# Two linear-attention and MLP layers on one core: the first tile's mean from two engines, two tiles by halves, and five new instruction lists

## The chip, the cores and the metric

The kernel runs on one core of a Trainium2 chip. A core has five engines with an instruction stream of their own each: TensorE (PE in the profile) multiplies matrices into eight PSUM banks, VectorE (DVE), ScalarE (ACT) and GpSimd (POOL) do elementwise work, and SyncE (SP) issues most of the DMAs. The engines wait for each other only by semaphores. The metric is the device time of one execution in microseconds. The kernel before takes 326.31 us, the median of 3 runs (325.96 to 327.42).

## The reference

`x` is 2048 tokens by 512 channels, in bf16. Two attention blocks alternate with two MLP blocks, and both layers share the same weights:

```
phi = lambda t: where(t > 0, t + 1, exp(t)) + 1e-6
def A(x):                                  # linear attention, 32 heads of 16
    q, k, v = split(x @ wqkv)              # wqkv: 512 x 1536
    pq, pk = phi(q), phi(k)
    kv  = einsum("bhsd,bhse->bhde", pk, v)
    z   = einsum("bhsd->bhd", pk)
    num = einsum("bhqd,bhde->bhqe", pq, kv)
    den = einsum("bhqd,bhd->bhq", pq, z)[..., None] + 1e-6
    return (num / den) @ wo                # wo: 512 x 512
def B(x):                                  # MLP, 512 -> 1792 -> 512
    return gelu(layernorm(x) @ w1 + b1) @ w2 + b2

x = x + A(layernorm(x));  x = x + B(layernorm(x))
x = x + A(layernorm(x));  x = x + B(layernorm(x))
```

`layernorm` subtracts the mean over the 512 channels and divides by `sqrt(var + 1e-5)`.

## The kernel before

The 2048 tokens are 16 tiles of 128, in four chunks of four tiles. Chunk 3 (tiles 12 to 15) is worked first, then chunks 0, 1 and 2. Every piece of work is an operation with a name, an engine, the keys that it reads and writes, and the buffers it uses. For each engine the configuration at the top of the file (`ORDER` in `CONF`, line 345) holds a list of all its operations by name, written out; the engines run these lists in that order, and a planner (`Scheduler`, line 114) only goes through them with estimated durations to give buffers to the operations. `WAY` says for some operations which engine or method does them. A wait is put in wherever an operation reads what another engine, or a DMA, has still to write, or takes a buffer that another has still to give up. So the five lists set which work can overlap, and an operation whose turn has not come waits even if its data are there.

In the names the first digit is the layer (0 or 1; in the names of the first norm it stands behind A, in those of the second behind B), the last ones are the tile, or the chunk and a part. What stands around the change:

- DMA loads on SP: `x0` (tiles 12 and 13), `wk0` and `wk1` (the two halves of the q and k weights, split along the 512 channels that are summed over), `x2` (tiles 14 and 15), then `xc0` to `xc2` (the other chunks). `wv`, `wo` and four pieces of `w1` and `w2` follow later on GpSimd's queue.
- `norm` (line 713). A tile's mean and variance come from two VectorE instructions, `stats` (bn_stats, line 741, over 512 channels) and `aggr` (line 743). `veps` adds eps, `pow` (GpSimd, line 756) raises to -1/2. For tiles 12 to 15 of layer 0 the mean is subtracted at once (`cen`, line 722, into the buffer `yb`), and the tile goes on to its transpose without 1/std; that factor (`rstd`) is applied where q and k are read out of PSUM, and to `yb` itself later, by `ysc` (lines 763 and 766). The other tiles have both in one instruction, `norm` (line 776 on ScalarE, with `nmr` ahead of it on GpSimd; line 781 on VectorE).
- The transpose: `PT` is four TensorE transposes (`transpose_pe`, line 795) and `tc` the copy out of PSUM; tile 12's are done by halves, two transposes and a copy each (lines 804 and 811). Other tiles go by a DMA transpose (`TA`, `TB`, `TP` on SP, lines 791 and 1120).
- `K0_t` and `Q0_3_k` are the k and q projections of a tile, four matmuls of 128 x 128 by 512 each (lines 878 and 908). For tile 12 they are two pairs (`K0_12_0` then `K0_12`, line 887; `Q0_3_0_0` then `Q0_3_0`, line 917), the first for the first half of the weights. `Q` of chunks 0 and 1 in layer 0 works on all four tiles of a chunk (line 934).
- phi of a projection: `exp` and `relu` on ScalarE (lines 848 and 859), `min` and `phi` on VectorE (lines 861 and 865; lines 852 and 854 where phi is a maximum and no relu is needed), some `phi` on GpSimd.
- `G` multiplies the normed tile by phi(k) (line 1004, in four PSUM banks that are held for all of layer 0), so that K and Q have the other four banks until then. `za` adds phi(k) for z on GpSimd (zacc, line 957); `zhi`, `zlo` and `ZH` (lines 963, 966 and 973) turn it into a column; `Z` does the same for whole chunks (line 985). `cpg`, `KV`, `kvm`, `M` and `cpm` make one 512 x 512 matrix of it all, `D`, `ln`, `rec`, `pr` divide by the denominator, `WO` (line 1152) multiplies, and `RA` adds the residual.
- `statsB` to `normB` is the second norm; `W1Lc_f_h` the up-projection of a chunk (line 1184; chunk 0 by halves of two tiles), `gelu` on ScalarE (line 1190), `W2L_t_0` and `W2L_t_7` the two halves of a tile's down-projection (line 1223), `RB` the residual, `OD` the store.

Between `exp` and `gelu` ScalarE loads another table (line 1356), 11 times in the list before. At the start TensorE runs matmuls on constants (`warm`, line 703), and a few more between the first transposes (`idle0_0` and `idle0_1`, as many as `N_IDLE` says).

Of the kernel before, what the change touches and what calls it, by code (L numbers as in the profile page):

```python
# [7 lines left out]
ACT = mybir.ActivationFunctionType  # L8
ALU = mybir.AluOpType

P = 128
# [271 lines left out]
def assign_waits(graph, order, sems, dma_sems):  # L283
# [10 lines left out]
    while len(done) < total:  # L294
        moved = False
        for e in ENGINES:
# [43 lines left out]
    N_WARM2=9, N_IDLE=[2, 1], XQ='sp', WKQ='sp sp', WK1=1, K_SPLIT=1, K_HALVES=(0, 1), X_HEAD=((0, 2), (2, 2)),  # L340
# [204 lines left out]
def build_kernel(nc, A_x, A_wqkv, A_wo, B_x, B_w1, B_b1, B_w2, B_b2, out, conf=None, report=False):  # L545
# [5 lines left out]
    with ExitStack() as es:  # L551
# [161 lines left out]
        def norm(src, src_keys, src_tiles, double, on_act, prio, tag, src16=False, head=False):  # L713

            s = Tile(STATS, f"st{tag}")
            k = f"st{tag}"
            by_act = eng(f"st{tag}") == "act"
            centred = eng(f"cen{tag}") is not None

            def centre(mean, op):  # L720
                y = Tile(YB, f"y{tag}")
# [698 lines left out]
```

## Time and profile before

| what | us |
|---|---|
| median of 3 runs (lowest, highest) | 326.31 (325.96, 327.42) |
| the profiled execution's own time | 326.6 |
| its span, from the first to the last instruction | 324.9 |
| busy in the span: TensorE | 319.8 |
| busy: VectorE | 224.4 |
| busy: ScalarE | 193.7 |
| busy: GpSimd | 144.6 |

The granted clock is 1.00 in all of the span. Matmuls overlap in the array, and a matmul's end is modelled, so TensorE's busy time counts some standing still; the starts of its matmuls are the better measure. Times in the timeline count from the span's start. In the answer by stretches the columns are the stretch and its length, the busy time and instructions of TensorE's matmuls, its weight loads, VectorE, ScalarE and GpSimd, then the granted clock, the DMA engines' share and GB/s. An idle time in square brackets stands before the instruction, with what ended it.

### The profile page before, as it was taken

How to read it: one execution, taken by the hardware profiler on the slowest of the kernel's cores; microseconds unless marked ns; L12 is line 12 of the kernel's file. 1: busy time of each engine (PE TensorE's matmuls, PEld its weight loads, DVE VectorE, ACT ScalarE, POOL GpSimd, SP SyncE). 2: the span in 40 equal slices, each digit the busy share in tenths (PEclk: the TensorE clock that was granted, in tenths of full speed). 3: DMA queues.
4: the chain of work that ended last, by engine and by line, in shares of the span. 5: the costliest groups of instructions: out<-in, count | busy, mean ns of one | idle time of the engine just before them, and what ended most of it. 6: DMA issues, size and time to landing. Idle time of an engine off the chain costs nothing.

```text
span 324.9 us, 4758 instructions
## 1 busy us (share of the span) xinstructions
PE 319.8 (98%) x1703; PEld 157.9 (49%) x1703; DVE 224.4 (69%) x508; ACT 193.7 (60%) x333; POOL 144.6 (45%) x231
## 2 busy tenths in 40 slices
PE   7999999999999999999999999999999999999996
PEld 3444445567444444444444444558644444444443
DVE  4998979997998854003779999899899666100032
ACT  3999699745253235899527656978934734563300
POOL 4699476646522862500346825755904543100000
PEclk9999999999999999999999999999999999999999
DMA  7343179003331221210110300121230421300012
GB/s 259 144 64 72 40 236 355 18 16 76 40 64 35 58 57 32 43 22 17 34 33 16 67 17 0 18 48 36 41 72 18 82 65 50 81 0 15 31 65 69
DMA packets 46355, 20.37 MB, mean 63 GB/s; under 512 B 42044, under 2 KB 44220, under 8 KB 46332
## 3 DMA queue, kind: packets, MB, share of 16 engines
q1 hardware_dynamic: 45132, 15.32, 20.6%
q0 software_dynamic: 1056, 4.72, 4.1%
q8 instruction: 13, 0.21, 0.3%
q14 instruction: 10, 0.08, 0.1%
q10 hardware_dynamic: 144, 0.03, 0.0%
HBM read 8.00 MB, written 2.10 MB: 31 GB/s over the span
## 4 chain that ended last, share of the span: by engine, by line
PE 88%; DVE 4%; POOL 3%; DMA 2%; issue 1%; ACT 0%; SPq 0%
PE ps L1184 30%; PE ps L1223 29%; PE ps L1152 9%; PE ps L878 5%; PE ps L1036 4%; PE ps L908 4%; PE ps L1004 2%; PE ps L934 2%; DMA t<-in_A_x_dram 2%; DVE stats L741 1%; POOL rstd L756 1%; PE ps L1210 1%; PE ps L1128 1%; POOL zacc L957 1%; DVE yb L781 1%
## 5 line engine op out<-in xcount | busy, mean ns | idle before, releaser
L1190 ACT ACTIVATE gT<-ps,b1c 128x512 bf16<-128x512 f32 (+1 forms) x140 | 76.9, 600 | 70.9 <-PE ps L1184 70.6
L1184 PE MATMUL ps<-t,w 128*128 128x512 bf16 (+1 forms) x560 | 102.6, 336 | 0.0
L1223 PE MATMUL ps<-w,gT 128*128 128x512 bf16 x434 | 98.2, 379 | 0.0
L1184 PEld LDWEIGHTS ps<-t,w 128*128 128x128 bf16 x560 | 54.5, 98 | 43.9 <-ACT t L833 0.6
L1223 PEld LDWEIGHTS ps<-w,gT 128*128 128x128 bf16 x434 | 42.5, 98 | 50.5 <-ACT gT L1190 0.2
L848 ACT ACTIVATE eb<-ps 128x512 bf16<-128x512 f32 x56 | 32.8, 608 | 17.2 <-PE ps L878 10.6
L756 POOL TENSOR_TENSOR rstd<-veps,neghalf 128x1 f32<-128x1 f32 x64 | 38.7, 615 | 5.6 <-DVE veps L754 3.2
L1233 DVE TENSOR_TENSOR pkb<-ps,xsb 128x512 bf16<-128x512 f32 x15 | 10.0, 682 | 32.8 <-PE ps L1223 32.7
L741 DVE BATCH_NORM_STATS2 stats<-xsb 128x6 f32<-128x512 f32 x48 | 32.2, 681 | 0.2
L878 PE MATMUL ps<-wqkv,t 128*128 128x512 bf16 x124 | 31.2, 379 | 0.0
L1229 DVE TENSOR_TENSOR xsb<-ps,xsb 128x512 f32<-128x512 f32 x16 | 10.9, 686 | 29.2 <-PE ps L1223 29.2
L1152 PE MATMUL ps<-gtb,t 128*128 128x512 bf16 x128 | 30.7, 379 | 0.0
L754 POOL TENSOR_SCALAR veps<-mv 128x1 f32<-128x1 f32 x29 | 8.3, 297 | 39.1 <-DVE mv L743 38.4
L859 ACT ACTIVATE rb<-ps 128x512 bf16<-128x512 f32 x38 | 22.7, 612 | 2.0 <-PE ps L878 1.5
L776 ACT ACTIVATE yb<-xsb,nmr,rstd 128x512 bf16<-128x512 f32 x21 | 16.8, 812 | 10.8 <-POOL nmr L773 10.8
L781 DVE TENSOR_SCALAR yb<-xsb,mv,rstd 128x512 bf16<-128x512 f32 x27 | 15.3, 574 | 10.1 <-POOL rstd L756 9.9
L1169 POOL TENSOR_TENSOR xsb<-xsb,b2b 128x512 f32<-128x512 f32 x14 | 17.6, 1258 | 5.4 <-DVE yb L781 4.9
L1116 POOL TENSOR_TENSOR t<-t,rr 128x512 bf16<-128x512 bf16 x7 | 7.7, 1100 | 26.2 <-DVE rr L1112 16.5
L746 POOL TENSOR_SCALAR veps<-mv 128x1 f32<-128x1 f32 x32 | 10.2, 319 | 20.6 <-DVE mv L743 18.8
L1152 PEld LDWEIGHTS ps<-gtb,t 128*128 128x128 bf16 x128 | 12.4, 98 | 14.0
L908 PE MATMUL ps<-wqkv,t 128*128 128x512 bf16 x76 | 19.2, 379 | 0.0
L878 PEld LDWEIGHTS ps<-wqkv,t 128*128 128x128 bf16 x124 | 11.8, 98 | 14.5 <-ACT rb L859 0.6
(102 smaller groups left out, 415.9 us busy)
## 6 DMA issues: line engine op xcount, KB each, us to landing
w<-in_B_w_dram POOLq DMA_DIRECT2D x4, 896.0 KB, 7.2
out_dram<-pkb SPq DMA_DIRECT2D x15, 128.0 KB, 2.0
t<-in_A_x_dram SPq DMA_DIRECT2D x3, 512.0 KB, 7.3
wqkv<-in_A_wqkv_dram SPq DMA_DIRECT2D x2, 512.0 KB, 4.6
t<-yb SPq DMA_TRANSPOSE x56, 2.5
t<-in_A_x_dram SPq DMA_DIRECT2D x2, 256.0 KB, 4.2
wqkv<-in_A_wqkv_dram POOLq DMA_DIRECT2D x1, 512.0 KB, 4.4
wo<-in_A_wo_dram POOLq DMA_DIRECT2D x1, 512.0 KB, 5.1
```

What stands on the lines that cost most here:

```text
L741: G.op("dve", lambda e: e.bn_stats(stats[:, s.slot, :], src()), 602, reads=src_keys, writes=[k + "s"], tiles=[s, *src_tiles], prio=prio, n ...
L756: G.op("pool", lambda e: e.tensor_tensor(rstd[:, s.slot:s.slot + 1], veps[:, s.slot:s.slot + 1], neghalf[:], op=ALU.pow), 530, reads=[k + ...
L781: G.op("dve", lambda e: e.tensor_scalar(yb[:, y.slot, :], src(), stats[:, s.slot, 2:3] if by_act else mv[:, s.slot, 0:1], rstd[:, s.slot:s ...
L848: G.op("act", lambda e: e.activation(eb[:, et.slot, :], bank(bt), ACT.Exp, scale=factor()), 569 if by else 483, reads=[src_key, *more], wr ...
L859: G.op("act", lambda e: e.activation(rb[:, rt.slot, :], bank(bt), ACT.Relu, scale=factor()), 569 if by else 478, reads=[src_key, *more], w ...
L878: ins = e.matmul(bank(b), lhsT=yTa(yT)[:, dt, k * P:(k + 1) * P], rhs=wqkv[:, dt, D:2 * D], start=(dt == 0), stop=(dt == DT - 1))
L908: ins = e.matmul(bank(b), lhsT=yTa(yT)[:, dt, k * P:(k + 1) * P], rhs=wqkv[:, dt, 0:D], start=(dt == 0), stop=(dt == DT - 1))
L1152: ins = e.matmul(bank(wb), lhsT=yTa(pq)[:, kt, k * P:(k + 1) * P], rhs=gtb[:, kt, :], start=(kt == 0), stop=(kt == DT - 1))
L1169: G.op("pool" if on_pool else "dve", lambda e: e.tensor_tensor(xsb[:, st, :], xsb[:, st, :], b2b[:], op=ALU.add), 1120 if on_pool else 600 ...
L1184: ins = e.matmul(bank(b, n), lhsT=w1[:, dt, ft * P:(ft + 1) * P], rhs=yTa(yT)[:, dt, k0 * P:k1 * P], start=(dt == 0), stop=(dt == DT - 1))
L1190: G.op("act", lambda e, ft=ft, b=b, k0=k0, k1=k1, n=n: e.activation(gT[:, g.slot, ft * 512 + k0 * P:ft * 512 + k1 * P], bank(b, n), ACT.Ge ...
L1223: ins = e.matmul(bank(b), lhsT=gT[:, g.slot, ft * 512 + k * P:ft * 512 + (k + 1) * P], rhs=w2[:, ft, :], start=(ft == 0), stop=(ft == FT - 1))
```

## The change

Three settings of the configuration change: `K_SPLIT` from 1 to 2, `N_IDLE` from `[2, 1]` to `[4, 1]`, and `WAY` has `stA0_12` as "both" and `stA0_13` as "sum" (it was "dve" for tile 13).

With "both", tile 12's mean is taken ahead of its statistics: ScalarE sums channels 256 to 511 (`sumA0_12`, a copy that also accumulates), VectorE sums channels 0 to 255 (`redA0_12`), VectorE adds the two and multiplies by -1/512 (`negA0_12`), and the mean is added to the tile by two instructions of 256 channels each (`cenA0_12_0`, `cenA0_12_1`), so that each half can be transposed by itself. With "sum", ScalarE sums all of tile 13 (`sumA0_13`), VectorE scales it (`negA0_13`), and one `cen` follows. `stats`, `aggr`, `veps` and `pow` come after that in both and serve for `rstd` alone. `K_SPLIT=2` makes tile 13's projections two pairs of matmuls as well (`K0_13_0`, `K0_13`, `Q0_3_1_0`, `Q0_3_1`).

The five lists are replaced. On TensorE 390 names become 392, on ScalarE 322 become 324, on VectorE 508 become 512; GpSimd's and SP's hold the same names in another order. All other names are the same, permuted. The start of TensorE's list, and the code:

```diff
-    N_WARM2=9, N_IDLE=[2, 1], XQ='sp', WKQ='sp sp', WK1=1, K_SPLIT=1, K_HALVES=(0, 1), X_HEAD=((0, 2), (2, 2)),
+    N_WARM2=9, N_IDLE=[4, 1], XQ='sp', WKQ='sp sp', WK1=1, K_SPLIT=2, K_HALVES=(0, 1), X_HEAD=((0, 2), (2, 2)),
...
-            "warm PTA0_12_0 PTA0_12_1 idle0_0 PTA0_13 idle0_1 K0_12_0 K0_12 Q0_3_0_0 Q0_3_0 K0_13 PTA0_14 Q0_3_1 "
-            "PTA0_15 K0_14 G0_12_0 K0_15 Q0_3_2 Q0_3_3 G0_13_0 PTA0_1 K0_0 G0_14_0 K0_1 G0_15_0 G0_0_0 K0_3 K0_2 "
...
+            "warm PTA0_12_0 PTA0_12_1 idle0_0 Q0_3_0_0 PTA0_13 idle0_1 Q0_3_0 K0_12_0 K0_12 Q0_3_1_0 Q0_3_1 K0_13_0 "
+            "PTA0_14 K0_13 PTA0_15 K0_14 K0_15 Q0_3_3 G0_12_0 G0_13_0 Q0_3_2 K0_0 PTA0_1 G0_14_0 K0_3 K0_1 G0_15_0 "
+            "G0_0_0 K0_2 Q0_0_0 Q0_0_3 G0_1_0 Q0_0_2 G0_2_0 K0_10 K0_8 K0_5 K0_4 G0_3_0 Q0_0_1 K0_6 K0_7 K0_9 G0_4_0 "
+            "Q0_1_3 K0_11 Q0_1_2 ZH0 G0_5_0 Z0_1 Z0_2 Q0_1_1 Q0_1_0 D0_0_3 G0_6_0 D0_0_0 G0_7_0 G0_8_0 D0_0_1 G0_9_0 "
...
-        "pz1_3_1": "dve", "pz1_3_2": "pool", "pz1_3_3": "pool", "stA0_13": "dve", "tc_10": "act", "tc_11": "dve",
+        "pz1_3_1": "dve", "pz1_3_2": "pool", "pz1_3_3": "pool", "stA0_12": "both", "stA0_13": "sum", "tc_10": "act", "tc_11": "dve",
...
+            early = eng(f"st{tag}") if eng(f"st{tag}") in ("both", "sum") else None
...
+                if early == "both":
+                    halves = cf["K_HALVES"]
+                    n = D // len(halves)
+                    G.parts[f"y{tag}"] = tuple(f"y{tag}_{h}" for h in halves)
+                    for h in halves:
+                        cs = slice(n * h, n * h + n)
+                        G.op("dve", lambda e, cs=cs: e.tensor_scalar(yb[:, y.slot, cs], src()[:, cs], mean(), None, op0=op), 180,
...
-            if by_act:
+            if early:
...
+                h0 = D // 2 if early == "both" else 0
+                G.op("act", lambda e: e.activation(eb[:, et.slot, h0:D], src()[:, h0:D], ACT.Copy, accum_out=st6(0)), 450 if h0 else 630,
...
+                if h0:
+                    G.op("dve", lambda e: e.tensor_reduce(st6(3), src()[:, 0:h0], axis=mybir.AxisListType.X, op=ALU.add), 330, reads=src_keys,
...
+                    G.op("dve", lambda e: e.tensor_scalar(st6(2), st6(0), st6(3), -1.0 / D, op0=ALU.add, op1=ALU.mult), 75,
...
+                else:
+                    G.op("dve", lambda e: e.tensor_scalar(st6(2), st6(0), -1.0 / D, None, op0=ALU.mult), 75,
...
+                y = centre(lambda: st6(2), ALU.add)
+                G.op("dve", lambda e: e.bn_stats(stats[:, s.slot, :], src()), 602, reads=src_keys, writes=[k + "s", k + "t", k + "m"],
...
-                    o = G.op("pe", turn, n * 66, reads=[ykey, f"id{P}"], writes=[f"{key}_{h}p"], tiles=[bs[h], y], prio=prio, name=f"PT{tag}_{h}",
+                    o = G.op("pe", turn, n * 66, reads=[f"{ykey}_{h}" if ykey in G.parts else ykey, f"id{P}"], writes=[f"{key}_{h}p"], tiles=[bs[h], y], prio=prio, name=f"PT{tag}_{h}",
...
-                    if f"yT{L}_{4 * c + k}" in G.parts:
+                    if L == 0 and c == HC and k < cf["K_SPLIT"]:
```

The other places that the prediction speaks of, in the new lists:

- VectorE begins with `ones redA0_12 negA0_12 cenA0_12_0 cenA0_12_1 negA0_13 statsA0_12 cenA0_13 aggrA0_12 vepsA0_12 statsA0_13 aggrA0_13 yscA0_12 statsA0_14`; `yscA0_13` stands behind `aggrA0_1`. Further on it has `normA0_11 mink0_4 phik0_4 minq0_0_1 mink0_5 mink0_7 phik0_5 mink0_6 phik0_7 zhi0 mink0_9 zlo0`.
- ScalarE begins with `sumA0_12 sumA0_13 tcA0_12_0 tcA0_12_1 tcA0_13 reluq0_3_0 expq0_3_0 reluk0_12 expk0_12 tcA0_14 expk0_13 tcA0_15`. It has 9 table changes. At the end of layer 1's first chunk it has `gelu1_0_4_1 normB1_6 gelu1_0_9_1 gelu1_0_2_1 normB1_4 gelu1_0_6_1 expq1_2_2 expq1_2_3 gelu1_0_10_1 normB1_7`, where the list before had `gelu1_0_6_0 normB1_4 gelu1_0_10_1 gelu1_0_5_1 expq1_2_3 expq1_2_2 gelu1_0_0_1 gelu1_0_8_1 normB1_6 normB1_7`.
- TensorE there goes `W11_0_9_1 W21_1_0 W21_0_0 W21_1_7 W21_0_7 W21_3_0 W21_3_7 WO1_12_0 W11_1_13_0`; before it did four tiles of `W21` and three `WO` ahead of `W11_1`.
- GpSimd: `bdm0` stands between `vepsA0_13` and `powA0_13` (it was first), `bdm1` behind `za0_1` (it was fifth), `b1z` behind `pr0_1_0`, and the DMA `w1_1` behind `pr0_1_1`.
- SP: the seven loads come first as before; then `TA0_0 TA0_3 TA0_2 TA0_5 TA0_10 TA0_8 TA0_4 TA0_7 TA0_6 TA0_9 TA0_11 b1 Tb1 TB0_1 TB0_3 TB0_2 b2` (before: `b1` behind `TA0_8`, `b2` ahead of `TB0_1`).

More of the change, by code (lines that the diff above doesn't have):

```diff
@@ L724, in centre @@
                 return y
[L725 removed]
+            if early:
+                et = Tile(EB, f"sq{tag}")
+                st6 = lambda i: stats[:, s.slot, i:i + 1]
+                h0 = D // 2 if early == "both" else 0
+                G.op("act", lambda e: e.activation(eb[:, et.slot, h0:D], src()[:, h0:D], ACT.Copy, accum_out=st6(0)), 450 if h0 else 630,
+                     reads=src_keys, writes=[k + "s"], tiles=[s, et, *src_tiles], prio=prio, name=f"sum{tag}", lat=90)
+                if h0:
+                    G.op("dve", lambda e: e.tensor_reduce(st6(3), src()[:, 0:h0], axis=mybir.AxisListType.X, op=ALU.add), 330, reads=src_keys,
+                         writes=[k + "t"], tiles=[s, *src_tiles], prio=prio, name=f"red{tag}", lat=40)
+                    G.op("dve", lambda e: e.tensor_scalar(st6(2), st6(0), st6(3), -1.0 / D, op0=ALU.add, op1=ALU.mult), 75,
+                         reads=[k + "s", k + "t"], writes=[k + "m"], tiles=[s], prio=prio, name=f"neg{tag}", lat=40)
+                else:
+                    G.op("dve", lambda e: e.tensor_scalar(st6(2), st6(0), -1.0 / D, None, op0=ALU.mult), 75,
+                         reads=[k + "s"], writes=[k + "m"], tiles=[s], prio=prio, name=f"neg{tag}", lat=40)
+                y = centre(lambda: st6(2), ALU.add)
+                G.op("dve", lambda e: e.bn_stats(stats[:, s.slot, :], src()), 602, reads=src_keys, writes=[k + "s", k + "t", k + "m"],
+                     tiles=[s, *src_tiles], prio=prio, name=f"stats{tag}", lat=50)
+                G.op("dve", lambda e: e.bn_aggr(mv[:, s.slot, :], stats[:, s.slot, :]), 92, reads=[k + "s"], writes=[k + "a"],
+                     tiles=[s], prio=prio, name=f"aggr{tag}", lat=55)
+                head = eng(f"veps{tag}") == "dve"
+                G.op("dve" if head else "pool",
+                     lambda e: e.tensor_scalar(veps[:, s.slot:s.slot + 1], mv[:, s.slot, 1:2], EPS, None, op0=ALU.add),
+                     75 if head else 182, reads=[k + "a"], writes=[k + "v"], tiles=[s], prio=prio, name=f"veps{tag}", lat=50)
+            elif by_act:
                 et = Tile(EB, f"sq{tag}")
```

10 lines of the change are left out of this document (7 added, 3 removed), and 268 rows, old and new, of the table ORDER.

## The prediction

> **What bounds the kernel now.** I read the page's busy line first, then the busy time by stretches, then TensorE's own timeline, and then, for each place where TensorE stood still, the waits.
>
> ```profile
> PE 319.8 (98%) x1703; PEld 157.9 (49%) x1703; DVE 224.4 (69%) x508; ACT 193.7 (60%) x333; POOL 144.6 (45%) x231
> ```
>
> ```profile
> 12.00:16.00 4.00, 4.00 (x20) 1.79 (x19) 3.97 (x11) 4.00 (x9) 3.70 (x7) 1.00 0.16 33
> 20.00:25.00 5.00, 5.00 (x25) 2.27 (x24) 4.93 (x15) 4.92 (x9) 4.54 (x10) 1.00 0.34 69
> 30.00:35.00 5.00, 4.30 (x21) 1.69 (x19) 4.76 (x8) 2.75 (x6) 3.83 (x5) 1.00 0.33 67
> 60.00:100.00 40.00, 40.00 (x245) 23.40 (x244) 36.15 (x80) 20.46 (x42) 19.20 (x25) 1.00 0.26 47
> ```
>
> TensorE (first busy column) is full; until 35 us VectorE and ScalarE (third and fourth) are nearly full beside it, later they have room. A busy TensorE may still lose time, so I go by the starts of its matmuls:
>
> ```profile
> 5.34 0.57 PE L804 MATMUL ps<-idp,yb 128*128 128x128 bf16 x4 [0.40 <-DVE yb L722]
> 5.74 0.28 PE L697 MATMUL ps<-const-bfloat16-1.0 128*128 128x128 bf16 x2
> 5.86 0.38 PE L823 MATMUL ps<-idp,yb 128*128 128x128 bf16 x4
> 6.21 0.60 PE L887 MATMUL ps<-wqkv,t 128*128 128x512 bf16 x2
> 7.40 0.59 PE L887 MATMUL ps<-wqkv,t 128*128 128x512 bf16 x2 [0.58 <-DMA wqkv<-in_A_wqkv_dram]
> 7.83 1.03 PE L917 MATMUL ps<-wqkv,t 128*128 128x512 bf16 x4
> 8.69 1.03 PE L878 MATMUL ps<-wqkv,t 128*128 128x512 bf16 x4
> 9.75 0.40 PE L823 MATMUL ps<-idp,yb 128*128 128x128 bf16 x4
> ```
>
> ```profile
> 33.16 1.03 PE L878 MATMUL ps<-wqkv,t 128*128 128x512 bf16 x4
> 34.89 0.39 PE L1004 MATMUL ps<-pkb,yb 128*128 128x512 bf16 x1 [0.70 <-DVE pkb L854]
> ```
>
> From 7.83 to 8.69 four 512-wide matmuls take 0.86 us: the pace is 0.216 each. At that pace the two at 6.21 end at 6.64, but the next start at 7.40: 0.75 us waiting for the second half of the weights (wk1). The four at 8.69 end at 9.55 and tile 14's transposes start at 9.75: 0.20 lost. The four at 33.16 end at 34.02 and the next start at 34.89: 0.86 lost. Going so through the whole timeline I find four losses of 0.04 to 0.08 between 19 and 33 us (0.26), and 0.06 at 74.3; after that none. So past 7.40 TensorE loses 1.38 us in all; before 7.40 it has done 0.43 us of matrix work (K0_12's first half) and some transposes.
>
> ```profile
> PE ps L1004 <- DVE pkb L854: 0.7, 1, 0.7
> PE ps L887 <- DMA wqkv<-in_A_wqkv_dram: 0.6, 1, 0.6
> ```
>
> Behind the longest loss stands VectorE: ahead of the one that TensorE waited for (L854), normA0_11 took 1.31 where its kind takes 0.41, while GpSimd added zacc (32.93 to 34.08). The last line is zlo0, which matters below:
>
> ```profile
> 32.92 1.31 DVE L781 TENSOR_SCALAR yb<-t,mv,rstd 128x512 bf16<-128x512 bf16 x1
> 34.15 0.68 DVE L854 SCALAR_TENSOR_TENSOR pkb<-ps,eb 128x512 bf16<-128x512 f32 x1
> 37.50 1.26 DVE L966 TENSOR_TENSOR eb<-zacc,dz 128x512 bf16<-128x512 f32 x1
> ```
>
> The sum is made against the profiled execution: span 324.9, device time 326.6, so 1.7 outside the span, 0.3 above the median 326.31.
>
> **1. The first tile's mean ahead.** Removed: the wait of cenA0_12 for both bn_stats and their aggregates (3.52 to 4.94). Added: sumA0_12 (ScalarE, 256 wide), redA0_12 (VectorE, 256 wide), two neg, one more cen, sumA0_13 (ScalarE, 512). None but cen is in the trace. sumA0_12: 0.38 by the 256-wide copy of L811, 0.82 by the 512-wide SBUF copy of L763; half of the latter, 0.41, is nearest. redA0_12: half of L1107's 0.675, 0.34, beside it; bounds 0.15 (smallest VectorE row) and 0.68. neg 0.15 each (L754). A cen half: 0.15 to 0.34 (L722). x lands at 3.52, so the first transposes could go at 4.2 to 4.9; TensorE's warm-up ends at 4.73, so 4.8 instead of 5.34. On VectorE the stats of 12 and 13 move behind, and cenA0_13 then ends at about 5.8, where TensorE took it before (5.86). **All of this is worth nothing**: Q0_3_0_0 runs at about 5.3 in place of K0_12_0, but the next in the list is Q0_3_0, the half that needs wk1, and nothing in the change moves that transfer, third on its queue in both. At 7.40 TensorE has again done one half of a projection. Cover: TensorE is through with all that stands ahead of Q0_3_0 by about 6.2, so the new path could be over 1 us slower before it cost. rstd of tile 12 comes at about 6.9 (one pow row, 0.6, after veps at 6.2), of tile 13 at 8.7, because bdm0 (0.86) now stands before its pow; the evictions that read them start at 8.03 and about 10.8.
>
> **2. From 7.40 to 35 us.** Q0_3_1, 0.86 of work, now stands ahead of tile 14's transposes: the loss at 9.55 goes, -0.20. But four evictions still precede tile 14's copy on ScalarE (8.03 to 10.32 before), so K0_14, due at 10.87 at pace, waits for a copy that ends at about 10.95, and K0_15 for one at 12.0, due 11.87: +0.13 and +0.2. yscA0_13 (0.35) moves from VectorE's idle time before 7.9 into its full stretch. VectorE's old stream up to zlo0's end (38.76) held 0.91 idle; the new one has 0.2 each for minq0_0_1 and mink0_9 and 0.35 for ysc more. Its end is 39.5 if all the idle returns and 38.6 if none does; adding the steps of the new list row by row I get 38.8, since each operand of ScalarE comes just before it is due. The ZH0 matmuls wait for zlo0: 38.9, with G0_5 and Z0_1 (0.86 and 0.40) still to do but Q0_1_2 (0.86) done. Before, ZH0 started at 39.63; for equal work that is 39.23. **So -0.3**, bounds -0.6 and +0.35: the loss at 34 becomes two of some 0.5, before G0_4 and ZH0. From there to the first up-projection the slack is thin, but no row says it is less than before: normB0_1 followed RA0_0 by 4.05 (55.18 to 59.23), has the same operations ahead of it now, and its transpose lands near 62.0, just when W10 is due.
>
> The queues. SP issues TA0_4 behind TA0_10 and TA0_8; normA0_4 ends near 26.9, the transpose (2.5) lands at 29.5 to 29.9, and K0_4 is due at 29.8: under 0.1, within the bounds. GpSimd: bdm1 moves behind za0_1 and delays za0_3 by 0.85, whose reader zhi0 had 1.4 to spare (34.08 to 35.49). b1z moves behind pr0_1_0, to about 50; SP's b1, Tb1 and TB0_1 queue behind it. b1 then lands near 52.5 and Tb1 near 55; TB0_1 is due at 59.5, b1c at 57: nothing. w1_1 moves behind pr0_1_1, from 47.6 to about 53.5; with the 4.8 that the lone w2_1 took it lands by 58.5, and is due at 62: nothing, and 3.5 us of delay before it costs. b2 moves behind TB0_2: it lands near 70, where b20_0 wants it.
>
> **3. From 35 us to the end.** The lists are permuted; the matmuls are the same ones, so their 313 us stay. Two table loads fewer stand in ScalarE's list (9 against 11 changes between exp and gelu): 2.6 us of ScalarE's idle time. The tail keeps its last steps, from W21_11_7 on. Lower bound of new losses: 0 (before: 0.06). Upper bound: 1.7, from the one place I found without margin (below). Nearest row: the lists that lose 0.06 here; but a list that lost 1.3 in the 30 us where VectorE was full, and has VectorE busy 55.6 of 60 us from 160 to 220, leaves more: I take 0.3.
>
> **Sum**: -0.3 + 0.3 = 0: 326.6 by the profiled execution, 326.3 against the median.
>
> **Rivals.** *Slower: W11_1 waits for tile 7 (second block).* Its first matmul moves from 245.31 to 239.2 + 1.3. Ahead of it ScalarE's list now has exp1_2_2 and exp1_2_3 between two table loads, a gelu and normB1_7.
>
> ```profile
> 232.07 1.28 ACT L1356 ACT_TABLE_LOAD   x1
> 233.37 1.08 ACT L848 ACTIVATE eb<-ps 128x512 bf16<-128x512 f32 x2
> 234.47 1.28 ACT L1356 ACT_TABLE_LOAD   x1
> 236.49 1.51 ACT L776 ACTIVATE yb<-xsb,nmr,rstd 128x512 bf16<-128x512 f32 x2
> ```
>
> By these rows that is 1.3 + 1.1 + 1.3 + 0.4 + 0.8 = 4.9, then 2.8 from the transpose's issue to the matmul (242.49 to 245.31 before): 7.7. TensorE gives 9.9 between the last up-projection of the first chunk and W11_1 (six halves of 1.51 and one WO). ScalarE has 2.2 for the three gelus and normB1_4 (2.1) still to come: margin 0.1. Beyond that each gelu it is behind (0.37, at most three, since one of the four buffers is held) and a late nmr for normB1_4 (0.52 before) cost in full: up to 1.6, and with the 0.1 to 0.3 of other losses **328.0**. For it: no margin. Against: ScalarE was within 0.5 us of TensorE at the end of that phase before.
>
> *Faster: all losses past 7.40 go* (-1.4, 324.9), and wk1 lands 0.4 earlier: **324.5**. For it: the two equal weight halves took 3.7 and 5.5 us to land, so the second is no fixed number. Against: VectorE stays full until 40 us.
>
> *A cold TensorE.* The four transposes at 5.34 take 0.10 each and those at 5.86 0.055: TensorE reaches full pace there. In the new list it idles from about 6.2 to 7.40, 1.2 us against 0.75. If it came out at half pace, every microsecond until it recovers loses half: 327.2 for 1.8 us of it, 328.0 for 3.4. For it: the longer gap; against: no slow matmul followed the 0.75 one. The Trainium skill, "TensorE: Matmul & The Clock Gate", Part 1, says that the clock halves after an idle window of about 3.4 us, free-running. By that rule a gap of 1.2 us is harmless; this trace agrees only for 0.75.
>
> **How the numbers follow.** Against the median, within 0.5% (1.6 us) is about what a measurement of this kernel can tell from no change. Losses re-dealt as summed: 0.48, with a range of its own from 325.7 to 327.3 (the bounds of step 2 and 1.0 in step 3). Slower rival and its like in the dense stretch: 0.32, of which 0.30 past 327.9. Faster rival: 0.14, of which 0.10 below 324.7. Cold TensorE: 0.06, of which 0.04 past. So faster 0.10, same 0.56, slower 0.34; the range 324.8 to 328.4 leaves out about 2 in 10.
>
> **What would show it.** First transposes near 4.8, but the first 512-wide matmul behind a wait for wk1 at about 7.4; no loss before tile 14, small ones before K0_14 and K0_15, then G0_4 and ZH0 (L973) waiting for VectorE; the first up-projection (L1184) near 62.0 instead of 62.34; W11_1 near 240.5. Wrong if the full pace starts well off 7.4, if L1184 waits anywhere for ScalarE's yb or a transpose, or if TensorE loses over 1 us between 62 and 322.

## The result and the profile after

The changed kernel takes 327.78 us (median of 12 runs, 327.33 to 329.86) beside 326.31 us for the kernel before (12 runs, 325.96 to 327.42): ratio 1.0046, 95% interval 1.0035 to 1.0057. It is slower by 1.47 us, just inside the 0.5% that the prediction called "same", and in the upper part of its range. One of the 12 times of a later measurement of the changed kernel (e9 below) is 1934.65 us; without it that median is 328.18 instead of 328.28. The profiled execution has a span of 326.0 us and a time of 327.72 us.

The busy line of the page has TensorE busy 1.5 us less in a span that is 1.1 longer, and GpSimd 4.5 us less; the other engines changed by 0.7 at most. TensorE's figure is to be read with care: 32 of its 1705 matmuls have no record here (its weight loads have all 1705), which lowers it.

```profile
PE 318.3 (98%) x1673; PEld 158.3 (49%) x1705; DVE 224.1 (69%) x512; ACT 193.0 (59%) x335; POOL 140.1 (43%) x231
```

TensorE's waits in the changed kernel (total us, times, longest) have three rows that the kernel before did not have. They name three different releasers: VectorE, a DMA and ScalarE.

```profile
PE ps L1042 <- DVE pkb L903: 1.1, 1, 1.1
...
PE ps L916 <- DMA t<-yb: 0.7, 1, 0.7
PE ps L955 <- DMA wqkv<-in_A_wqkv_dram: 0.5, 1, 0.5
PE ps L916 <- ACT t L871: 0.3, 1, 0.3
```

TensorE's own timeline has the places (start, busy us, instruction; in brackets what ended the wait):

```profile
7.00 0.59 PE L955 MATMUL ps<-wqkv,t 128*128 128x512 bf16 x2 [0.49 <-DMA wqkv<-in_A_wqkv_dram]
...
17.15 1.03 PE L1042 MATMUL ps<-pkb,yb 128*128 128x512 bf16 x4
18.91 1.46 PE L916 MATMUL ps<-wqkv,t 128*128 128x512 bf16 x6 [0.74 <-DMA t<-yb]
...
29.27 1.93 PE L916 MATMUL ps<-wqkv,t 128*128 128x512 bf16 x8
32.28 1.04 PE L1042 MATMUL ps<-pkb,yb 128*128 128x512 bf16 x4 [1.08 <-DVE pkb L903]
```

Read by starts and at 0.216 us a matmul, as the prediction does: the four at 17.15 (G0_14) end at 18.01 and K0_3 starts at 18.91, 0.90 lost to a DMA transpose. The eight at 29.27 end at 31.0 and G0_3 starts at 32.28, 1.24 lost to VectorE. With 0.21 before K0_14 and 0.19 before K0_15 (ScalarE's copies) and 0.32 in small ones, TensorE loses 2.86 us past the start of full pace; the kernel before loses 1.40 by the same reading (1.38 in the prediction). That is 1.46 more. The start is 0.40 earlier (7.00 against 7.40, since wk1 landed earlier in this execution): 1.46 - 0.40 gives the span's 1.1. The 1.46 alone is close to the medians' 1.47, but the starts of the executions that were not profiled are not on record.

The operand of G0_3 is phik0_3, on VectorE, and GpSimd worked beside it. In the kernel before the two are these rows:

```profile
26.20 0.46 DVE L865 TENSOR_TENSOR pkb<-eb,rb 128x512 bf16<-128x512 bf16 x1
```

```profile
29.63 1.03 PE L1004 MATMUL ps<-pkb,yb 128*128 128x512 bf16 x4
```

In the changed kernel, VectorE first, then GpSimd:

```profile
26.98 1.28 DVE L890 TENSOR_SCALAR eb<-eb 128x512 bf16<-128x512 bf16 x1 [0.30 <-ACT eb L886]
...
30.85 1.38 DVE L903 TENSOR_TENSOR pkb<-eb,rb 128x512 bf16<-128x512 bf16 x1
```

```profile
26.96 1.15 POOL L995 TENSOR_TENSOR zacc<-zacc,pkb 128x512 f32<-128x512 f32 x1
...
30.64 1.30 POOL L995 TENSOR_TENSOR zacc<-zacc,pkb 128x512 f32<-128x512 f32 x1
```

Two things are to be seen. phik0_3 starts at 30.85; before, it followed mink0_3 at 26.20, and now twelve more operations stand between the two. And it takes 1.38 where the same form takes 0.42 elsewhere, while the addition za0_1 runs; minq0_0_3 at 26.98 takes 1.28 instead of 0.28 beside za0_0.

### The profile page after: what moved, and what is told of

It is laid out like the page before. It is cut to its first block, busy times and chain, and to the rows that moved or that the text cites. A ratio compares the mean times of both kernels' runs of the same rounds, so it can differ in the third digit from the quotient of the medians.

```text
span 326.0 us, 4730 instructions
## 1 busy us (share of the span) xinstructions
PE 318.3 (98%) x1673; PEld 158.3 (49%) x1705; DVE 224.1 (69%) x512; ACT 193.0 (59%) x335; POOL 140.1 (43%) x231
## 4 chain that ended last, share of the span: by engine, by line
PE 89%; DVE 4%; DMA 3%; ACT 2%; issue 1%; SPq 0%; ACTq 0%
PE ps L1222 29%; PE ps L1261 29%; PE ps L1190 8%; PE ps L916 6%; PE ps L946 4%; PE ps L1074 4%; PE ps L1042 3%; PE ps L972 2%; DMA t<-in_A_x_dram 2%; DVE stats L778 1%; DMA t<-yb 1%; PE ps L1248 1%; PE ps L1166 1%; ACT eb L886 1%; ACT yb L814 1%
## 5 line engine op out<-in xcount | busy, mean ns | idle before, releaser
L1228 ACT ACTIVATE gT<-ps,b1c 128x512 bf16<-128x512 f32 (+1 forms) x140 | 77.8, 601 | 77.5 <-PE ps L1222 76.8
L793 POOL TENSOR_TENSOR rstd<-veps,neghalf 128x1 f32<-128x1 f32 x64 | 39.5, 622 | 7.6 <-DVE veps L760 4.7
L916 PE MATMUL ps<-wqkv,t 128*128 128x512 bf16 x117 | 29.0, 379 | 1.1 <-DMA t<-yb 0.7
L783 POOL TENSOR_SCALAR veps<-mv 128x1 f32<-128x1 f32 x32 | 7.5, 234 | 50.4 <-DVE mv L780 48.9
L791 POOL TENSOR_SCALAR veps<-mv 128x1 f32<-128x1 f32 x28 | 7.2, 267 | 40.2 <-DVE mv L780 39.4
L946 PE MATMUL ps<-wqkv,t 128*128 128x512 bf16 x69 | 18.0, 379 | 0.2
L1207 POOL TENSOR_TENSOR xsb<-xsb,b2b 128x512 f32<-128x512 f32 x14 | 16.8, 1206 | 0.7 <-DMA b2b<-in_B_b_dram 0.6
L1042 PE MATMUL ps<-pkb,yb 128*128 128x512 bf16 x63 | 15.9, 379 | 1.1 <-DVE pkb L903 1.1
```

Source lines behind the costliest of these rows:

```text
L793: G.op("pool", lambda e: e.tensor_tensor(rstd[:, s.slot:s.slot + 1], veps[:, s.slot:s.slot + 1], neghalf[:], op=ALU.pow), 530, reads=[k + ...
L916: ins = e.matmul(bank(b), lhsT=yTa(yT)[:, dt, k * P:(k + 1) * P], rhs=wqkv[:, dt, D:2 * D], start=(dt == 0), stop=(dt == DT - 1))
L946: ins = e.matmul(bank(b), lhsT=yTa(yT)[:, dt, k * P:(k + 1) * P], rhs=wqkv[:, dt, 0:D], start=(dt == 0), stop=(dt == DT - 1))
L1042: ins = e.matmul(ps[:, gb.slot + dc, :], lhsT=yb[:, y.slot, dc * P:(dc + 1) * P], rhs=pkb[:, pk.slot, :], start=(st == FIRST), stop=(st == ...
L1228: G.op("act", lambda e, ft=ft, b=b, k0=k0, k1=k1, n=n: e.activation(gT[:, g.slot, ft * 512 + k0 * P:ft * 512 + k1 * P], bank(b, n), ACT.Ge ...
```

## The experiments

**How to compare.** wk1 lands at another time in each profiled execution (6.7 to 8.1 us), so a span alone misleads by up to 1 us. I take the *remainder*: span less the start of the half projection that waits for wk1 (K0_12 before, Q0_3_0 in the changed kernel; TensorE has done one half projection by then in both). Edits are written as moves: `_move("dve", "a", "b")` takes a out of VectorE's list and puts it right behind b.

| run | ratio to the kernel before [95%] | start | span | remainder | wait before K0_3 | before G0_3 |
|---|---|---|---|---|---|---|
| before | 1 | 7.40 | 324.9 | 317.5 | 0 | 0 |
| changed | 1.0046 [1.0035, 1.0057] | 7.00 | 326.0 | 319.0 | 0.90 | 1.24 |
| e5, changed again | 1.0014 [1.0003, 1.0025] | 7.09 | 326.1 | 319.0 | 0.84 | 1.32 |
| e9, changed, third | 1.0033 [1.0018, 1.0047] | 6.98 | 325.9 | 318.9 | 0.86 | 1.11 |
| e1, phik0_3 early | 1.0001 [0.998, 1.0021] | 7.04 | 324.7 | 317.7 | 0.94 | 0 |
| e2, K0_3 late | 1.0020 [0.9999, 1.0041] | 7.03 | 325.3 | 318.3 | 0 | 0.81 |
| e3, lists without the mean | 1.0019 [0.9999, 1.0039] | 7.06 | 325.3 | 318.2 | 0 | 1.36 |
| e4, mean without the lists | 1.0001 [0.998, 1.0021] | 7.34 | 324.8 | 317.5 | 0.58 | 0 |
| e6, zacc late | 1.0093 [1.0075, 1.0111] | 7.08 | 328.4 | 321.3 | 0.91 | 1.42 |
| e10, zacc short | 1.0008 [0.9992, 1.0024] | 8.24 | 326.4 | 318.2 | 0.92 | 0.48 |
| e11, normA0_3 early | 1.0011 [0.9997, 1.0025] | 6.95 | 325.7 | 318.8 | 0 | 1.36 |
| e7, phik0_3 and normA0_3 early | 0.9989 [0.9973, 1.0004] | 7.43 | 325.1 | 317.7 | 0 | 0 |
| e8, e7 and the head | 1.0002 [0.9988, 1.0017] | 8.16 | 326.5 | 318.3 | 0 | 0 |
| e12, e7 and G0_12 | 0.9980 [0.9964, 0.9996] | 7.87 | 325.2 | 317.3 | 0 | 0 |
| e16, e12 again | 0.9988 [0.9973, 1.0003] | 6.90 | 324.6 | 317.7 | 0 | 0 |

e1 to e4, e5 to e8, e9 to e12, e13 to e16 and the last two (e17 and e18) were each on a chip of their own, beside the kernel before. e13 to e15, e17 and e18, which are not in the table, are the kernel before itself and two variants of its warm-up; they come last.

**e1: phik0_3 back to an early place.**

```diff
+_move("dve", "phik0_3", "normA0_4")
```

> The changed kernel with one operation moved: in VectorE's list phik0_3 stands right behind normA0_4 (where it has 0.30 us of idle time behind it) in place of 12 operations later. TensorE's list is untouched. Theory A (the place of phik0_3 in the list causes the 1.24 us that TensorE waits before G0_3): that wait goes, G0_4 and ZH0, now due 1.24 us earlier, take back 0.2 to 0.6 of it, because their operands end on VectorE at about 35.2 and 39.0; time 0.6 to 1.0 below the changed kernel, 326.8 to 327.2. Rival B (VectorE beside GpSimd's zacc additions is too slow whatever the order; the stretch falls on another operation): the wait turns up in full before G0_4 or ZH0, time 327.6 to 327.9. The 0.90 before K0_3 stays in both.

326.81 us; the kernel before beside it 326.97. VectorE's row of phik0_3 and TensorE's of G0_3 in this run:

```profile
26.63 0.42 DVE L913 TENSOR_TENSOR pkb<-eb,rb 128x512 bf16<-128x512 bf16 x1
```

```profile
31.07 1.03 PE L1052 MATMUL ps<-pkb,yb 128*128 128x512 bf16 x4
```

The wait before G0_3 is gone whole, and nothing came back before G0_4 or ZH0, where I had allowed 0.2 to 0.6: the remainder falls by 1.3. The stretch by zacc fell on other operations (normA0_11 1.35, minq0_3_2 0.75), whose readers had time. Theory A holds: the place in the list is enough to take the wait away. The 0.94 before K0_3 is still there, and the remainder is within 0.2 of the kernel before all the same.

**e2: K0_3 back behind G0_0.**

```diff
+_move("pe", "K0_3", "G0_0_0")
```

> The changed kernel with one operation moved: on TensorE K0_3 stands behind G0_0 again, as in the kernel before, in place of ahead of K0_1. Its transpose lands at 18.78 us, K0_3 is then due near 20.6. Theory A1 (the wait for the transpose costs in full): the 0.90 goes, time 0.9 below the changed kernel, 326.9. Rival B1 (VectorE sets the pace here, and TensorE runs into its operands anyway): phik0_15 ends at 19.22 and phik0_0 at 20.41, where G0_15 and G0_0 would now be due at 18.87 and 19.73, so 0.4 and 0.3 of the 0.90 turn up there, and what is left is lost before G0_3, whose operand does not come earlier: time 327.6 to 327.8.

327.54 us. The 0.90 is gone; 0.11, 0.31 and 0.30 stand before K0_1, G0_15 and G0_0, and G0_3 waits 0.81. The four make 1.53 against 2.14 in the changed kernel: 0.6 of the 0.9 is a gain, between the two theories. The moved order also made the planner give many matmuls other PSUM banks, so the 0.81 may not be of this move alone.

**e3 and e4: the two halves of the change apart.** e3 is the changed kernel's lists without the early mean, e4 the early mean in the kernel before's lists. The edits to the lists are written here in short, by names taken out and put in:

```diff
 e3: changed kernel
+CONF["WAY"]["stA0_12"] = CONF["WAY"]["stA0_13"] = "dve"
 scalar: -sumA0_12 -sumA0_13
 vector: ones -redA0_12 -negA0_12 -cenA0_12_0 -cenA0_12_1 -negA0_13
         +statsA0_12 +statsA0_13 +aggrA0_12 +aggrA0_13 +cenA0_12 +cenA0_13 +vepsA0_12 yscA0_12 ...
 e4: kernel before, with the changed kernel's code
+CONF["WAY"].update(stA0_12="both", stA0_13="sum")
 scalar: +sumA0_12 +sumA0_13 tcA0_12_0 ...
 vector: ones +redA0_12 +negA0_12 +cenA0_12_0 +cenA0_12_1 +negA0_13 statsA0_12 cenA0_13 ...
+_move("dve", "yscA0_13", "normA0_0")
 gpsimd: neghalf, then powA0_12 vepsA0_13 powA0_13 ahead of the rest
```

> The changed kernel's five lists without the early mean: tile 12's and 13's means come from bn_stats again, as before; sumA0_12, sumA0_13, redA0_12 and the negs are gone, all else of the lists is as changed. Theory A (the lists' dense stretch from 17 to 33 us holds the loss): the first transposes start at about 5.4 in place of 4.7, nothing else moves, since TensorE waits for wk1 until about 7; time 327.6 to 328.0, with the waits before K0_3 and G0_3 as in the changed kernel. Rival C (the early mean costs by itself, through ScalarE's two sums or the later statistics of tiles 12 and 13): 326.3 to 327.2.

> The kernel before with the early mean alone: sums on ScalarE, redA0_12, the negs and the halved centring ahead of the statistics; TensorE's and SP's lists as before, the pow rows of tiles 12 and 13 first on GpSimd, yscA0_13 behind normA0_0 on VectorE. Theory A: the first transposes start at 4.7 and TensorE waits for wk1 as before; time 326.1 to 326.6, the losses of the kernel before in their places. Rival C (the early mean costs by itself): 327 to 327.8.

e3: 327.65 us, e4: 326.89, the kernel before 326.97 beside both. By the remainder the mean alone costs nothing (317.5) and the lists alone cost 0.7 (318.2), yet together they cost 1.5: they are not independent. What differs is the wait before K0_3. In e3, with the same place of K0_3 and the same issue time (15.35 against 15.29), tile 3's transpose lands in 2.5 us and nothing waits. In e4, with the old lists, it takes 4.6 and K0_3 loses 0.58; there G0_4 then waits only 0.14, so the loss is paid once. My expectation of e3 had the time right and the place wrong.

**What makes one transpose slow.** The DMA view of the changed kernel from 15.28 to 18.79 us (queue, kind, packets, MB, share), and its one transpose issued at 15.29 (issues, median us to landing), then the same issue in e3 and in e2. In the kernel before the transpose of tile 3, issued at 16.77, has the same line as in the changed kernel, 3.5.

```profile
q14 instruction: 1, 0.01, 0.6%
...
t<-yb SPq DMA_TRANSPOSE x1, 3.5
```

```profile
t<-yb SPq DMA_TRANSPOSE x1, 2.5
```

```profile
t<-yb SPq DMA_TRANSPOSE x1, 4.9
```

By its name the queue "instruction" carries the engines' own code, here one packet of 8 KB. In the changed kernel it starts at 17.13 and takes 0.35 us, in the middle of the transpose's packets; in e3 at 17.64, when they are through. In e2 a second one, 16 KB on queue q8, starts at 17.59 and takes 1.55. Over the 20 profiles of this study, 1237 DMA transposes of 128x512 tiles during which no such packet ran took 2.39 to 2.56 us from issue to landing, without exception; the 283 with one took 2.4 to 4.9. Where a single 8 KB packet ran, its start tells the slow ones from the others: the 24 transposes in which it started 1.72 to 1.95 us behind the issue took 3.04 to 3.52, the 44 in which it started 2.19 us behind it or later took 2.41 to 2.56, and the 62 in which it started by 1.18 took 2.40 to 2.77. Counted from the start of full pace, the 8 KB packet comes at 10.1 to 10.4 us in all twelve profiles of the changed lists with the mean in them, and at 10.6 in e3, the one without it. At tile 3's transpose, where it is issued as in the changed kernel, that puts the packet 1.8 to 1.9 us behind the issue with the mean and 2.3 in e3, on the two sides of that edge. That the mean's added instructions pull the packet forward is argued and not shown: there is one profile without the mean, and no record of whose code the packet is.

The Trainium skill, "Runtime: NRT & Kernel Launch", section "Instruction fetch mechanics", says that each engine streams its code in blocks by DMA while it runs, and that the cost is mostly hidden. The trace agrees on the streaming (23 instruction packets in the changed kernel's span); the cost here shows in a transpose that is under way at that time, up to 2.3 us (4.88 in e2 against 2.56 at most without a packet).

**e11 and e7: the transpose issued earlier.** e11 is the changed kernel with the first three moves, e7 has the fourth as well.

```diff
+_move("act", "normA0_3", "reluk0_14")
+_move("dve", "minq0_3_1", "mink0_14")
+_move("dve", "phik0_14", "mink0_14")
 e7 besides:
+_move("dve", "phik0_3", "normA0_4")
```

> The changed kernel with normA0_3 behind reluk0_14 on ScalarE (and phik0_14, minq0_3_1 behind mink0_14 on VectorE), so that tile 3's transpose is issued earlier, but phik0_3 in its late place. Theory F: the wait of 0.9 before K0_3 goes, whether a fetch falls into the transpose or not. Theory B1 (VectorE sets the pace from there on): the wait before G0_3 grows by 0.1 to 0.6, since G0_3 is due earlier and phik0_3 not as much; time 0.3 to 0.8 below the changed kernel. Rival: the gain is the full 0.9, G0_3's wait stays at 1.24.

> The changed kernel with phik0_3 behind normA0_4 (as in the first run) and normA0_3 earlier on ScalarE, behind reluk0_14 in place of behind expq0_3_1, so that tile 3's transpose is issued near 14.1 in place of 15.3; on VectorE phik0_14 and minq0_3_1 follow mink0_14. K0_3 keeps its new place on TensorE. Theory F: the transpose lands by 16.6, or by 17.7 if the fetch still falls into it, both ahead of the 17.8 at which K0_3 is due: the 0.9 goes. VectorE's operands for G0_15 and G0_0 (19.25, 20.4) are then due at 19.8 and 20.6, and zlo0 for ZH0 at 37.9: 0 to 0.3 comes back. Time 0.6 to 0.9 below the run with phik0_3 alone moved, 0.5 to 0.9 below the kernel before. Rival B1 (VectorE sets the pace up to 40 us): all but 0.3 of it is lost again before G0_15, G0_0 or ZH0.

e11: 327.54 us, 0.74 below the changed kernel beside it (328.28). K0_3 waits for nothing, and G0_3's wait is 1.36 against 1.11: theory F for K0_3, B1 for what followed. By the remainder the gain is far less than 0.74, only 0.1 to 0.2 (318.8), since 0.50 now stands before tile 14's transposes. e7: 326.80 us, 1.03 below the changed kernel on that chip (327.83) and level with e1. I had expected 0.6 to 0.9 below e1. The 0.94 before K0_3 is gone, and 0.29 before tile 14's transposes, 0.11 before K0_4, 0.29 before Q0_0_1 and 0.13 before ZH0 have come in its place. The busy time of e7 from 9 to 38 us (stretch, length; TensorE, its weight loads, VectorE, ScalarE, GpSimd; clock, DMA share, GB/s) says why:

```profile
9.00:38.00 29.00, 28.68 (x140) 12.59 (x139) 28.52 (x82) 27.33 (x49) 23.75 (x45) 1.00 0.32 76
```

VectorE (third) has 0.48 of 29 us free. What is mended on TensorE's side beyond that only meets VectorE later: rival B1. So what the wait before K0_3 is worth depends on what else stands: without it the remainder is 0.7 lower in e2 and e3 (with other banks in e2, without the mean in e3), 0.1 to 0.2 lower in e11, and in e7 no lower than in e1.

**e6 and e10: is zacc's contention needed?**

```diff
 e6:
+_move("pool", "za0_0", "bdm1")
+_move("pool", "za0_1", "za0_0")
 e10: changed lists, in attn_z
-lambda e, second=second, k=k: e.tensor_tensor(zacc[:], ... zacc[:], pkb[:, pks[k].slot, :],
+lambda e, second=second, k=k, w=64 if L == 0 and st in (0, 1) else 512: e.tensor_tensor(zacc[:, 0:w], ... zacc[:, 0:w], pkb[:, pks[k].slot, 0:w],
```

> The changed kernel with two of GpSimd's operations moved: za0_0 and za0_1 stand behind bdm1 (from 26.96 and 30.64 to about 30.7 and 31.9 us); VectorE's list is as changed. In the changed kernel minq0_0_3 took 1.28 and phik0_3 1.38 while these two ran, against 0.28 and 0.42 to 0.68 for the same form elsewhere, together 1.7 to 2.0 us. Theory C (the 1.24 before G0_3 is this stretch): phik0_3 ends near 30.3 and the wait goes, although phik0_3 keeps its late place; some of it, up to 0.5, comes back before G0_4 or ZH0, since the additions now run there; time 0.7 to 1.2 below the changed kernel. Rival P (the place alone, 12 operations later, makes it late): 0.9 to 1.2 of the wait stays, time within 0.3 of the changed kernel.

> The changed kernel, its lists unchanged, with GpSimd's additions za0_0 and za0_1 cut from 512 columns to 64, so that they take about 0.3 us in place of 1.15 (the sum over the keys then lacks most of tiles 0 and 1: this part of the computation is left out). Theory C (contention is needed for the 1.24 before G0_3): minq0_3_2 and phik0_3 take 0.28 and 0.42 in place of 0.77 and 1.36, phik0_3 ends near 31.0 and the wait before G0_3 falls to 0 to 0.4; time 0.8 to 1.3 below the changed kernel. Rival P (the late place alone makes it): phik0_3 starts no earlier than 30.9, and 0.8 or more of the wait stays.

e6 missed on all counts: 330.49 us, and G0_3 waits 1.42. The additions only changed which operation they meet: mink0_8 took 0.92 beside bdm1 and phik0_3 1.36 beside za0_0. Worse, the planner hands out PSUM banks as it lays out the lists, and this order gave 490 of 1705 matmuls another bank. TensorE then waited between 54 and 70 us, far from the moved operations, for banks that VectorE had still to empty:

```profile
PEld ps L1201 <- DVE xsb L1206: 1.8, 3, 1.3
```

So e6 decides nothing on contention. (e1, e3, e7, e10 and e11 kept every bank; e2, e8 and e12 did not, with 1035, 159 and 12 matmuls.) e10 is the clean one: 327.68 us, 0.6 below the changed kernel beside it, and the wait before G0_3 falls to 0.48, from 1.11 to 1.32 in the three profiles of the changed kernel. I expected 0 to 0.4; it is more because phik0_3 still takes 1.05, now beside bdm1, GpSimd's mask operation, and no longer beside the short za0_1, which has just ended. VectorE, then GpSimd:

```profile
31.62 1.05 DVE L903 TENSOR_TENSOR pkb<-eb,rb 128x512 bf16<-128x512 bf16 x1
```

```profile
31.07 0.48 POOL L995 TENSOR_TENSOR zacc<-zacc,pkb 128x64 f32<-128x64 f32 x1
31.50 0.93 POOL L689 TENSOR_SCALAR_AFFINE_SELECT bdmask<-bdmask 128x512 bf16<-128x512 bf16 x1
```

Both causes are needed for the whole 1.24: an early place removes it with the contention left on (e1), less contention removes 0.6 to 0.85 of it in the late place. No run has the late place without any contention; as an estimate from these rows, phik0_3 at 0.42 in place of 1.05 would be 0.63 earlier and take away the last 0.48 too.

**e8 and e12: further than the changed kernel.** Both start from e7.

```diff
 e8:
+_move("dve", "aggrA0_14", "statsA0_14")
+_move("dve", "cenA0_14", "aggrA0_14")
+_move("pe", "PTA0_14", "Q0_3_1")
+_move("act", "tcA0_15", "tcA0_14")
+_move("dve", "mink0_13", "statsA0_1")
 e12:
+_move("dve", "phik0_12", "aggrA0_3")
+_move("pe", "G0_12_0", "K0_14")
```

> The run above with the head mended too: on VectorE tile 14's aggregate and centring ahead of tile 15's statistics, on TensorE tile 14's transposes half a projection earlier, on ScalarE tile 15's copy ahead of expk0_13, and on VectorE mink0_13 behind statsA0_1. Theory: the waits of 0.21 before K0_14 and 0.19 before K0_15 go; expk0_13 is 0.57 later, which costs VectorE's stream up to 0.1. Time 0.2 to 0.4 below the run above. Rival B1 (VectorE sets the pace up to 40 us): the 0.4 turns up before G0_15, G0_0 or ZH0, and the time is that of the run above.

> The run with phik0_3 behind normA0_4 and normA0_3 early, and besides G0_12 ahead of K0_15 on TensorE, as in the kernel before, with phik0_12 ahead of statsA0_0 on VectorE, so that K0_15 no longer waits 0.19 for tile 15's copy. Theory: that wait goes and nothing else moves; time 0.1 to 0.3 below the run without it, 0.997 to 0.999 of the kernel before. Rival B1 (VectorE, busy without a break from 9 to 38 us, sets the pace): the 0.19 comes back before Q0_0_1 or ZH0.

> The version with phik0_3 and normA0_3 early and G0_12 ahead of K0_15, a second time. If its gain is its own and not the chance of one chip: 0.996 to 0.9995 of the kernel before, remainder from the start of the full pace 317.3 within 0.2, against 317.5 of the kernel before. Rival: no difference, 0.999 to 1.001.

e8: 327.27 us, above e7 (326.80). K0_14's wait is 0.13 and K0_15's gone, but 0.35 before K0_0, 0.17 before PTA0_1, 0.25 before K0_8 and 0.24 before K0_4 are new: B1 again. e12: 326.55 us beside 327.21, and a second time 326.35 beside 326.58. K0_15's wait is gone; K0_0 and PTA0_1 together wait 0.2 to 0.4 instead. The first interval excludes 1, the second (0.9973 to 1.0003) does not. It is faster than the changed kernel on the same chip (328.28); against the kernel before the medians are 0.1 to 0.2% lower, and whether that is a gain is open. Its second remainder, 317.7, missed the 317.3 expected.

**e5, e9 and e13 to e18: how far behind is the changed kernel?** The ratio came out three ways.

> The changed kernel as it is, beside the kernel before on the same chip as the three runs that follow, and profiled a second time. Theory F (an instruction fetch, the 8 KB packet on queue q14 near 17.1 us, holds up tile 3's transpose): the fetch falls between the issue at 15.3 and the landing again, the transpose takes about 3.5 us in place of the 2.4 to 2.56 of all transposes without a fetch, and TensorE waits 0.9 before K0_3. Rival: the transpose is as slow without a fetch. Before G0_3 1.2 to 1.4 in both; ratio to the kernel before 1.003 to 1.006.

> The changed kernel as it is, beside the three runs that follow on the same chip, and a third profile of it. All theories: waits of 0.8 to 1.0 before K0_3 and 1.2 to 1.4 before G0_3. Open is how far it lies behind the kernel before, whose own times spread (1.0046 the first time, 1.0014 the second). Theory W (the spread is the landing of wk1, which starts the full pace anywhere from 7.0 to 8.2 us, in either kernel): span less the start of the full pace is the same as in its other two profiles within 0.2, and the ratio falls at 1.001 to 1.005. Rival: the rest of the span differs too.

> The kernel before, profiled a second time. Theory W: span less the start of the half projection that needs wk1 is 317.5 again, within 0.2, and only that start moves. Rival K (tile 3's transpose, due at 20.88 with 0.63 to spare, is at times held up further by an instruction fetch): K0_3 waits up to 0.6, as in the run with the mean alone, and the remainder is up to 318.1.

> The kernel before, profiled a third time; the same two theories: remainder 317.5 within 0.2 by W, up to 318.1 with a wait before K0_3 by K.

> The kernel before, profiled a fourth time; the same two theories.

All three intervals lie above 1. The changed kernel repeats itself: remainder 319.0, 319.0, 318.9, and the transpose took 3.48, 3.43 and 3.44 with the 8 KB packet in it each time. 1.0014 in e5 missed my 1.003 to 1.006. The changed kernel's median was the same there (327.83 against 327.78); what had moved is the kernel before, 327.12 against 326.31, with times from 326.38 to 328.36. Of its three further profiles two have remainders of 317.4 and 317.6 (325.95 and 326.62 us), as theory W says; K0_3 never waited, against rival K. The third took 328.19 us, has a remainder of 318.4 and shows neither. TensorE's timeline of it:

```profile
6.06 0.61 PE L804 MATMUL ps<-idp,yb 128*128 128x128 bf16 x4 [1.12 <-DVE yb L722]
...
7.20 1.91 PE L887 MATMUL ps<-wqkv,t 128*128 128x512 bf16 x4
8.91 1.66 PE L917 MATMUL ps<-wqkv,t 128*128 128x512 bf16 x4
10.41 0.81 PE L878 MATMUL ps<-wqkv,t 128*128 128x512 bf16 x3
```

x landed at 4.22 instead of 3.5, the first transposes came 1.4 us after the warm-up's last matmul, and the four matmuls at 7.20 need 1.71 us to the next row's start, 0.43 each: half pace, until about 10.4. So the cold TensorE of the prediction's third rival exists, in the kernel before. The Trainium skill, "TensorE: Matmul & The Clock Gate", Part 1, puts the switch to the full clock at the end of a busy window of about 3.4 us that runs freely; one window more, from 7 to 10.4, fits that, and so does another execution with the same late x (4.28) that was at full pace from 6.12 on.

> The kernel before with ten 512-wide warm-up matmuls in place of seven, so that TensorE is busy until about 5.3 to 5.9 us in place of 4.7, and the gap ahead of the first transposes (0.6 us where x lands at 3.5, 1.4 where it lands at 4.2) closes. The rest is unchanged; the transposes are up to 0.5 later, which wk1's wait covers. Theory H (the upper end of the kernel before's times is executions in which the gap keeps TensorE at half pace until about 10.4 us): the upper end goes, the highest of 12 is at most 1.3 above the lowest, the median 0 to 0.6 below the kernel before on this chip. Rival (the spread is wk1's landing alone): the spread stays near 2 us, the median the same or up to 0.3 higher.

> The kernel before with four 512-wide warm-up matmuls in place of seven: TensorE is idle from about 3.4 to 5.3 us or later. Theory H: half pace until about 10 us in most executions; four halves of 0.43 and the four transposes take twice as long, and the median is 1 to 2.3 us above the kernel before. Rival (spread is wk1's landing alone): the median the same within 0.3.

```diff
-N_WARM=7
+N_WARM=10   (e17; e18: N_WARM=4)
```

e17: 327.20 us beside 327.36, ratio 1.0006 [0.9988, 1.0025], eleven of twelve runs between 326.64 and 327.67 and one at 328.99, where the kernel before had 326.12 to 328.24. e18: 327.45 us, 1.0011 [0.9997, 1.0025], although its profile shows half pace from 7.5 to 10.5 us. Theory H asked for 1 to 2.3 us in e18: it falls as the explanation of the whole spread. What half pace behind wk1 costs an execution is seen in two profiles, e14 and e18: remainders of 318.4 and 318.5 against 317.5, about 1 us. In e18 it is not a late start: the first transposes, at 5.43, run at full pace (0.06 each), and the granted clock then reads 0.60, 0.50, 0.50 and 0.69 in the four microseconds from 7 to 11. Such a stretch makes an execution's mean clock 0.995, and that is on record for every one: 4 of 12 in e18, none of 12 in e17, and 9 of the 139 of the kernel before beside these runs, which lie 0.65 to 1.38 us above their chips' medians. That count misses starts like e14's, whose mean clock reads 1.00. How often those happen, and what else spreads the kernel before's times, stays open.

## Why the prediction was wrong

**Step 1** was right in its core. The first transposes start at 4.73 (said 4.8), the two halves of the first projection at 5.64 and 7.00 with the wait for wk1 between them, and the mean alone has the remainder of the kernel before. The added operations cost as estimated: sumA0_12 0.42, redA0_12 0.42, neg 0.15 to 0.21, two halves of cen 0.48. Not seen: each sum issues a second ScalarE instruction of 0.19 that reads out the accumulator, and the first transposes are at 4.73 only where x lands at 3.5; at 4.2 to 4.4 they start at 5.3 to 5.6.

**Step 2** failed: "So -0.3, bounds -0.6 and +0.35: the loss at 34 becomes two of some 0.5, before G0_4 and ZH0". G0_4 and ZH0 waited for nothing; K0_3 lost 0.90 and G0_3 1.24. The stretch made +1.2 (worked out under step 3), so the bounds failed too. Three things were missed in it.

- The move of K0_3 was never priced. Its transpose took 3.48 in the kernel before too (16.77 to 20.25, with 0.63 to spare); I used 2.5, the typical one, for the transposes I did price.
- VectorE's list was followed to its end at zlo0, but not to each operand on the way. phik0_3 went back by 4.7 us (26.20 to 30.85), while G0_3 became due only 1.4 later (29.63 to 31.04).
- Both bounds were taken from idle time alone. The contention with zacc had been read in the profile before (normA0_11, 1.31), yet the sum let the additions meet the same harmless operations again.

Right in it: K0_14 0.21 and K0_15 0.19 (said 0.13 and 0.2), the loss before tile 14's transposes gone (0.07 and 0.17 in the later profiles), K0_4 0.03 (under 0.1). Off without a wait of TensorE: b1's transpose was issued at 57.4 and landed at 59.9 (said near 55), w1_1 landed at 59.7 (said by 58.5), and zlo0 ended at 39.9 (said 38.8, at most 39.5).

**Step 3** was right: 0.3 from 35 us to the end, measured 0.30 (0.06 before KV0_3, 0.09 in WO0_0, 0.04 at 118.8, 0.10 at 174.8). Over the kernel before (0.06 there) that is +0.24, so of the +1.46 the stretch of step 2 made +1.2, where -0.3 was said.

**The rivals.** W11_1 waited for nothing; it starts at 241.67 (said 240.5 without the delay ahead of it), and the thin margin held. wk1 did land 0.4 earlier, as the "faster" rival had it, but that is the execution's, not the change's. The cold TensorE did not show in any of the three profiles of the changed kernel. The chance of 0.34 for slower stood on the wrong place: the wait that decided was in the stretch that I had called full on VectorE and in which I expected a gain.

**What would show it wrong** named losses past 62 us, a late start and waits of the up-projection; none of these came. The sign that did come is the time of the first up-projection: 63.34, where near 62.0 was said instead of 62.34. The list did not name a wait between 17 and 33 us, where the lists differ most.

## What to carry to other kernels

When an order is searched anew, list for every matmul the operand that moved most against it, and price that one by its own row, the slowest of its kind included; two operands came late here, and putting one of them back recovered 1.3 of 1.5 us. Where another engine is busy 28.5 of 29 us, mend its order first, because what is saved elsewhere can be lost again at its next operand, as in e7 and e8. Before comparing spans, take off the start that a load sets, and profile the kernel before more than once.

## What was not expected of the hardware

- A DMA transpose of a 128x512 tile took 2.39 to 2.56 us in 1237 of 1237 cases without an instruction packet in flight, and up to 4.88 with one; an 8 KB packet 1.72 to 1.95 us behind the issue made it 3.04 to 3.52, one from 2.19 us on left it at 2.41 to 2.56. The packets are 8 KB (0.3 to 1.3 us) and 16 KB (0.9 to 1.6 us).
- A TENSOR_TENSOR of two bf16 tiles took 1.36 to 1.38 instead of 0.42 beside a GpSimd addition, and 1.05 beside GpSimd's mask operation.
- Moving two GpSimd additions at 27 and 31 us cost 2.3 us of remainder, in waits between 54 and 70 us; the program's planner had given 490 matmuls other PSUM banks.
- The same program ran its first matmuls at half pace until about 6 us in one execution and until 10.4 in another. The second had a gap of 1.4 us before its transposes; a third, with 1.5 us, was at full pace from 6.12 on.
